# Part B's input rows by a plain transfer and a VectorE turn, with the late rows kept in SBUF

## The chip, the cores and the metric

The kernel runs on one core of a Trainium2 chip. The metric is the device time of one execution in microseconds. The core has a matrix engine (TensorE, PE in the profile, with its weight loads shown apart as PEld), VectorE (DVE), ScalarE (ACT), GpSimd (POOL) and SyncE (SP). All of them work on SBUF, which has 128 partitions; TensorE writes its sums to PSUM. Sixteen DMA engines move data between DRAM and SBUF. A transfer is issued from the instruction queue of one of the engines, here SyncE's or GpSimd's, and an engine that waits before issuing holds everything behind it in its queue.

## The reference

The output has two halves of 640 columns for 2048 tokens. Part A is a dilated sliding-window attention and is done first; the change touches its end only through a few copies. Part B is a recurrence over 64 segments of 32 tokens:

```python
for s in range(n_seg):                     # 64 segments, seg_len 32, memory of 8 rows
    xs = x[:, s * seg_len:(s + 1) * seg_len, :]
    h = concatenate([mem, xs], axis=1)     # 40 rows of 640
    q, k, v = h @ Wq, h @ Wk, h @ Wv       # 32 heads of 192
    p = softmax(where(mask, q k^T * scale, -1e9))
    o = (p v) @ Wo                         # 40 rows of 640
    mem = o[:, :8, :]
    outs.append(o[:, 8:, :])
```

All of it is bf16 with sums in fp32. The four weights of part B take 31.5 MB, more than SBUF holds. Each segment needs all of them, and needs the memory rows that the segment before it made.

## The kernel before, in words

Part B splits the 32 heads into four groups of eight. The weights are cut into units: for q, k and v a unit is 128 of the 640 input rows by the 1536 columns of a group, for the output weight a unit is 256 rows by 640 columns. Most units are loaded once and stay in SBUF. The 23 units per segment that `STREAMED` names are loaded anew in every segment into a ring of five buffers (`get_unit`, L387 to L395), from copies that part A made in DRAM. Their loads stand in SyncE's queue in the order of use; each waits until TensorE has read its buffer for the last time.

The 40 rows of a segment are split in an unusual way. 32 rows are "main": the 8 memory rows and the first 24 of the segment's x rows. The last 8 x rows are "late". A projection (`project32`, L445) multiplies 32 rows at a time, as stationary operand, with 384 weight columns, four column blocks side by side in the array. The late rows of four segments together make another block of 32 rows, "ahead". Since late rows don't depend on the memory, each weight group is projected for them only in one segment out of four (`RENEW`, and for q in `segment`, L640 to L650), for four segments at once. The result is turned on VectorE (`turn_late`, L472) and stored by GpSimd into small buffers, from which GpSimd later copies 8 columns per head into the q and k tiles (L491).

The input of a projection must have the 640 channels on partitions: a tile `HX` of 128 partitions, 5 channel blocks and 64 rows, 32 main and 32 ahead. There are two of these tiles, used in turn. To fill them, part A copies x in DRAM into `xwindows`, with 64 rows for every segment (`copy_windows`, L339): the 8 late rows of the segment before as placeholder for the memory, 24 main rows, and the 8 late rows each of four segments, placed so that the late rows of segment t always stand at position t modulo 4. `load_x(s)` (L429) is one transposing transfer of a window of 64 by 640 on SyncE's queue. It is called at the start of the segment before, and it stands between the loads of the last output units and those of the first k units.

At a segment's end the last group's output projection finishes in `Y`. Two engines copy it to `row` (L466, L467), TensorE turns the 8 memory rows (`memory_rows`, L592), and VectorE writes them over the placeholder in the next HX (L595). Only then can the next segment's first main projection start. In between TensorE projects ahead rows for q. The 32 other rows go out by two transfers on GpSimd's queue (L652). `row` shares its tile with the softmax values (`t` in the profile), so the first softmax of the next segment (L523) waits until the output transfer has read it.

TensorE's order in part B is the order of the program (`manual_schedule`, L657); the orders on the other engines are made by a scheduler. GpSimd also clears the old columns of P (L539) after the last turn of P in a segment.

Of the kernel before, what the change touches and what calls it, by code (L numbers as in the profile page):

```python
# [8 lines left out]
BF16 = mybir.dt.bfloat16  # L9
# [262 lines left out]
def part_b(ctx, tc, B_x, B_mem0, B_Wq, B_Wk, B_Wv, B_Wo, out, ident, n_seg, pre, nbuf, mid):  # L272
    nc = tc.nc
# [52 lines left out]
    def load_resident(units, engs):  # L326
        for k, u in enumerate(units):
            engs[k % len(engs)].dma_start(unit_tile(res[u], u), unit_src(u))
# [5 lines left out]
    respool = ctx.enter_context(tc.tile_pool(name="b_res", bufs=1))  # L334
    place_resident(respool, resident[:n_pre])
    dpool = ctx.enter_context(tc.tile_pool(name="b_copy", bufs=1, space=bass.MemoryType.DRAM))
    XW = dpool.tile([n_seg, 2 * SEG, Dm], BF16, name="xwindows")

    def copy_windows():  # L339

        rows = [(XW[0, 0:M], mem2[0:M]), (XW[0, M:SEG], x2[0:SEG - M])]
        for a, b in ((1, 49), (49, n_seg)):
            rows.append((XW[a:b, 0:SEG], x2[SEG * a - M:SEG * b - M].rearrange("(s n) d -> s n d", n=SEG)))
        groups = x2.rearrange("(t n) d -> t n d", n=SEG)[:, SEG - M:SEG]
        groups = groups.rearrange("(m k) n d -> k m n d", k=4)
        windows = XW[:].rearrange("(m k) n d -> k m n d", k=4)
        for r in range(4):
            for i in range(4):
                dst = windows[r][:, SEG + M * i:SEG + M * i + M]
                if i >= r:  # L350
                    rows.append((dst, groups[i]))
                else:
                    rows.append((dst[0:n_seg // 4 - 1], groups[i][1:n_seg // 4]))
                    rows.append((dst[n_seg // 4 - 1], groups[i][n_seg // 4 - 1]))
        for dst, src in rows:
            nc.sync.dma_start(dst, src)

# [10 lines left out]
        return ctx.enter_context(tc.tile_pool(name=name, reuse_waits="tile", **kw))  # L368

    xpool = pool("b_hx", bufs=1)  # L370
    HXs = [xpool.tile([128, 5, 64], BF16, name=f"HX{i}") for i in range(2)]
    wstream = pool("b_ws", bufs=nbuf)
    early = resident[n_pre:n_pre + 9]
    respool1 = pool("b_res1", bufs=1)
# [52 lines left out]
        (nc.scalar.copy if copies["n"] % 2 else nc.vector.tensor_copy)(dst, src)  # L427

    def load_x(s):  # L429
        if s < n_seg:  # L430
            nc.sync.dma_start_transpose(HXs[s % 2][:], XW[s])

    def main(s):
        return HXs[s % 2][:, :, 0:SEG]

    def ahead(s):
        return HXs[s % 2][:, :, SEG:2 * SEG]

    def columns(w, m, j):

# [4 lines left out]
    def project32(Xs, m, g, dcs=range(5), ps=None):  # L445

        if ps is None:
            ps = [ps_acc.tile([128, 384], FP32, tag="acc", name=f"acc{n}") for n in range(len(Xs))]
        for dc in dcs:
            w = get_unit((m, g, dc))  # L450
            for n, X in enumerate(Xs):
                for j in range(4):
                    nc.tensor.matmul(ps[n][32 * j:32 * j + 32, :], lhsT=X[:, dc, :], rhs=columns(w, m, j),  # L453
                                     start=(dc == 0), stop=(dc == 4), tile_position=(0, 32 * j))
        return ps
# [25 lines left out]
    def project_qk(s, m, g):  # L481
        T = tokens(QT if m == "q" else KT)
        renew = s == 0 or f"{m}{g}" in RENEW[s % 4]
        ps = project32([ahead(s), main(s)] if renew else [main(s)], m, g)
        if renew:
            turn_late(ps[0], m, g, s)
        sb = to_sb(ps[-1])

        def turns():
            b = late.pop((m, g, s))  # L490
            nc.gpsimd.tensor_copy(T[:, :, 32:L], b[:])  # L491
            free.append(b)
            turn(T[:, :, 0:32], sb)

        return turns

    def values(s, g):
        renew = s == 0 or f"v{g}" in RENEW[s % 4]
        ps = project32([ahead(s), main(s)] if renew else [main(s)], "v", g)
        for t, p in ((LV[g], ps[0]), (Vst, ps[-1]))[0 if renew else 1:]:  # L500
            v = t[:].rearrange("p (n e) -> p n e", e=64)
            w = bass.AP(v.tensor, v.offset, [v.ap[0], [256, 2], [1, 192]])
            evacuate(w, p[:].rearrange("p (h e) -> p h e", h=2))
# [55 lines left out]
    def mix(g, PT):  # L559

        ps = [ps_x.tile([128, 3, L], FP32, tag="x", name=f"OTps{a}") for a in range(4)]
        plan = [(late, half, k, col) for late in range(2) for half in range(2)
                for k, col in (((0, 0), (1, 128)), ((2, 320), (1, 192)))[half]]
        for n, (late, half, k, col) in enumerate(plan):
            V = LV[g] if late else Vst
            for a in range(4):
                nc.tensor.matmul(ps[a][:, k, :], lhsT=V[32 * a:32 * a + 32, col:col + 128],  # L567
                                 rhs=PT[32 * a:32 * a + 32, late, half, :],
                                 start=(n == 0), stop=(n == len(plan) - 1), tile_position=(32 * a, 0))
        for a in range(4):  # L570
            evacuate(OT[:, 3 * L * a:3 * L * a + 3 * L], ps[a][:].rearrange("p k n -> p (k n)"))

    def project_out(Y, g, pairs=range(6)):
        for a in pairs:
            i = 6 * g + a
            w = get_unit(("o", i, 0))
            for r in range(2):
                c = 2 * a + r
                for gv in range(2):
                    n = 640 * r + 320 * gv  # L580
                    nc.tensor.matmul(Y[64 * gv:64 * gv + 64, :], lhsT=OT[:, L * c:L * c + 64],  # L581
                                     rhs=w[:, n:n + 320], start=(i == 0 and r == 0), stop=(i == 23 and r == 1),
                                     tile_position=(0, 64 * gv))

    def memory_rows(s, Ysb):
        pt = ps_x.tile([128, 5, M], FP32, tag="x")
        for dc in (2, 0, 1, 3, 4):
            for gv in range(2):
                c0, c1 = max(128 * dc, 320 * gv), min(128 * dc + 128, 320 * gv + 320)
                if c0 < c1:  # L590
                    lo = c0 - 128 * dc
                    nc.tensor.matmul(pt[lo:lo + c1 - c0, dc, :], lhsT=Ysb[:, c0 - 320 * gv:c1 - 320 * gv],  # L592
                                     rhs=ident[:, 64 * gv:64 * gv + M], start=True, stop=True,
                                     tile_position=(0, lo))
        nc.vector.tensor_copy(HXs[(s + 1) % 2][:, :, 0:M], pt[:])  # L595

    def segment(s):
        last = s + 1 == n_seg
        load_x(s + 1)
        tq, tk, PT = {}, {}, {}  # L600
        tq[0] = project_qk(s, "q", 0)
        tk[0] = project_qk(s, "k", 0)
        tq[1] = project_qk(s, "q", 1)
        tq[0]()
        tk[0]()
        tk[1] = project_qk(s, "k", 1)
        put_p(s, 0, *softmax(scores(0)))
        tq[1]()
        tk[1]()
        tq[2] = project_qk(s, "q", 2)  # L610
        values(s, 0)
        soft = softmax(scores(1))
        tq[2]()
        PT[0] = turn_p()
        put_p(s, 1, *soft)
        tk[2] = project_qk(s, "k", 2)
        mix(0, PT[0])
        values(s, 1)
        tk[2]()
        PT[1] = turn_p()  # L620
        Y = ps_y.tile([128, 320], FP32, tag="y")
        project_out(Y, 0)
        put_p(s, 2, *softmax(scores(2)))
        tq[3] = project_qk(s, "q", 3)
        tk[3] = project_qk(s, "k", 3)
        mix(1, PT[1])
        values(s, 2)
        tq[3]()
        tk[3]()
        PT[2] = turn_p()  # L630
        project_out(Y, 1, range(0, 4))
        put_p(s, 3, *softmax(scores(3)))
        project_out(Y, 1, range(4, 6))
        mix(2, PT[2])
        values(s, 3)
        project_out(Y, 2, range(0, 4))
        PT[3] = turn_p(2)
        project_out(Y, 2, range(4, 6))
        mix(3, PT[3])
        if not last:  # L640
            gl = (s + 1) % 4
            ql = project32([ahead(s + 1)], "q", gl, range(0, 3))
        project_out(Y, 3)
        row = one.tile([128, 4, L], FP32, tag="t1")
        Ysb = row[:].rearrange("p a n -> p (a n)").bitcast(BF16)
        halves(Ysb, Y[:], 160)
        if not last:
            project32([ahead(s + 1)], "q", gl, range(3, 5), ql)
            memory_rows(s, Ysb)
            turn_late(ql[0], "q", gl, s + 1)  # L650
        for gv in range(2):
            nc.gpsimd.dma_start(out2[SEG * s:SEG * s + SEG, Dm + 320 * gv:Dm + 320 * gv + 320],  # L652
                                Ysb[64 * gv + M:64 * gv + L, :])

    load_x(0)
    load_resident(early, [nc.sync])
    with tc.manual_schedule(engines={mybir.EngineType.PE}):  # L657
        for s in range(n_seg):
# [71 lines left out]
```

## Time and profile before

| | |
|---|---|
| median of 3 runs | 2038.78 us (2033.06 to 2039.54) |
| profiled execution | 2035.72 us, span 2033.9 us |
| mean granted TensorE clock | 0.978 |
| busy: PE, DVE, ACT, POOL | 89%, 54%, 34%, 16% |
| DMA | 596 MB, 293 GB/s over the span |
| streamed loads per segment | 8 units of k, 5 of v (384 KB each), 10 of o (320 KB each) |
| median from issue to landing: k, v, o loads | 4.9, 5.0, 4.4 us |
| median from issue to landing: transpose of a window, output transfer | 4.6, 4.9 us |

Busy time says how much of the span an engine worked. A list of waits says for an engine and line what it waited for, how long in total, how often, and the longest wait. The chain is followed back from the last instruction and shows what set the end. An order of time shows single engines: start, length, line, operation, and in brackets the idle time before it and what ended it. SPq and POOLq are the instruction queues of SyncE and GpSimd, where issuing a transfer takes time too. The profile covers one execution; the shares are means over part A (the first 177 us) and the 64 segments.

### The profile page before, as it was taken

Reading aid. Unit: us, or ns where it says so; the run is one execution under the profiler, and the core shown is the slowest. Engines: PE = TensorE matmul, PEld = TensorE weight load, DVE = VectorE, ACT = ScalarE, POOL = GpSimd, SP = SyncE. Lnnn points to the kernel's source line nnn. Section 1 sums busy time; section 2 is a strip of 40 time slices with the busy share of each in tenths; the row PEclk is TensorE's granted clock in tenths of the full one; section 3 lists DMA queues with packets and bytes.
Section 4 is the critical chain, followed back from the end, with each engine's and each line's share of the span. In section 5 each row is a group of like instructions: output and inputs, shape, how many; then the busy total and the mean of one; then the engine's idle time right before and its main releaser. Section 6 shows DMA issues by size and latency. Waiting matters only on the chain.

```text
span 2033.9 us, 93689 instructions
## 1 busy us (share of the span) xinstructions
PE 1813.5 (89%) x40702; PEld 1136.7 (56%) x40702; DVE 1095.9 (54%) x3491; ACT 684.3 (34%) x1931; POOL 325.8 (16%) x1274
## 2 busy tenths in 40 slices
PE   7988888899888998999898988989898988998898
PEld 4655555555555555555555555555555554555555
DVE  5876455455555555555555455545554554455554
ACT  3544233333333333333333333333333332333332
POOL 2001111111111111121111111111111111111111
PEclk9999999999999999999999899999999999999999
DMA  9927998988999899999899899999998988999997
GB/s 345 305 76 271 311 292 298 296 296 295 292 301 311 292 300 304 315 304 303 297 310 307 277 294 306 311 290 298 301 304 291 302 289 280 295 291 305 309 301 261
DMA packets 270111, 596.07 MB, mean 293 GB/s; under 512 B 61065, under 2 KB 72841, under 8 KB 269385
## 3 DMA queue, kind: packets, MB, share of 16 engines
q1 hardware_dynamic: 264770, 585.97, 87.4%
q8 instruction: 319, 5.23, 1.0%
q0 software_dynamic: 4928, 4.11, 0.6%
q14 instruction: 94, 0.77, 0.1%
HBM read 576.85 MB, written 18.87 MB: 293 GB/s over the span
## 4 chain that ended last, share of the span: by engine, by line
PE 48%; DMA 26%; DVE 15%; issue 4%; ACT 4%; POOL 1%; SPq 1%; DVEq 0%; ACTq 0%; POOLq 0%
PE acc L453 21%; PE Y L581 16%; DMA t<-wcopy_o 11%; DMA out_dram<-row 7%; DMA t<-wcopy_v 3%; DVE QT L463 2%; PE OTps L567 2%; PE Sps L516 2%; DMA t<-wcopy_k 2%; DVE KT L463 2%; PE pq L95 2%; PE pt L550 2%; ACT sb L459 2%; DVE sm L531 1%; ACT t L529 1%
## 5 line engine op out<-in xcount | busy, mean ns | idle before, releaser
L453 PEld LDWEIGHTS <-HX 128*32 128x32 bf16 x19380 | 477.6, 97 | 324.2 <-issue 79.0
L581 PEld LDWEIGHTS <-OT 128*64 128x64 bf16 x6144 | 316.5, 110 | 175.6 <-issue 48.2
L459 ACT CAST sb<-acc 128x384 bf16<-128x384 f32 x646 | 298.5, 477 | 335.2 <-PE acc L453 295.3
L453 PE MATMUL acc<-wres_q,HX 128*32 128x384 bf16 x6460 | 335.4, 330 | 18.8 <-DVE HX L595 18.3
L581 PE MATMUL Y<-wres_o,OT 128*64 128x320 bf16 x3584 | 343.1, 303 | 7.6 <-DVE OT L427 7.6
L453 PE MATMUL acc<-t,HX 128*32 128x384 bf16 x4200 | 322.5, 335 | 29.6 <-DMA t<-wcopy_v 14.7
L581 PE MATMUL Y<-t,OT 128*64 128x320 bf16 x2560 | 282.3, 305 | 33.6 <-DMA t<-wcopy_o 28.0
L453 PE MATMUL acc<-wres_v,HX 128*32 128x384 bf16 x4844 | 285.8, 337 | 0.0
L529 ACT ACTIVATE t<-t 128x160 f32<-128x160 f32 x256 | 86.3, 337 | 493.3 <-DVE t L528 491.7
L523 DVE SCALAR_TENSOR_TENSOR t<-Sps,mask 128x160 f32<-128x160 f32 x256 | 81.6, 319 | 286.7 <-PE Sps L516 216.4
L453 PE MATMUL acc<-wres_k,HX 128*32 128x384 bf16 x3876 | 230.8, 334 | 0.0
L491 POOL COPY QT<-Lb 128x96 bf16<-128x96 bf16 x256 | 69.0, 269 | 862.9 <-PE Sps L516 862.9
L463 DVE STREAM_TRANSPOSE QT<-sb 128x384 bf16<-128x384 bf16 x256 | 144.2, 563 | 72.9 <-ACT sb L459 72.8
L427 DVE CAST OT<-OTps 128x120 bf16<-128x120 f32 x512 | 121.5, 265 | 77.2 <-PE OTps L567 76.9
L463 DVE STREAM_TRANSPOSE KT<-sb 128x384 bf16<-128x384 bf16 x256 | 143.9, 562 | 28.9 <-ACT sb L459 28.9
L516 PEld LDWEIGHTS <-QT 128*64 128x64 bf16 (+1 forms) x4096 | 120.1, 109 | 67.8 <-issue 39.8
L516 PE MATMUL Sps<-KT,QT 128*64 128x40 bf16 (+1 forms) x4096 | 137.1, 188 | 16.9 <-POOL KT L491 8.2
L479 POOL COPY Lb<-late 128x96 bf16<-128x96 bf16 x524 | 117.1, 270 | 165.9 <-DVE late L463 163.8
L531 DVE TENSOR_REDUCE sm<-t 128x4 f32<-128x160 f32 x256 | 81.2, 317 | 106.5 <-ACT t L529 106.5
L427 ACT CAST OT<-OTps 128x120 bf16<-128x120 f32 x512 | 107.6, 263 | 88.5 <-PE OTps L567 87.8
L550 PE MATMUL pt<-ident,P 128*128 128x128 bf16 x384 | 60.5, 230 | 63.5 <-DVE P L541 62.6
L463 DVE STREAM_TRANSPOSE late<-sb 128x384 bf16<-128x384 bf16 x134 | 76.7, 573 | 61.3 <-ACT sb L459 61.0
(77 smaller groups left out, 1543.4 us busy)
## 6 DMA issues: line engine op xcount, KB each, us to landing
t<-wcopy_o SPq DMA_DIRECT2D x640, 320.0 KB, 4.4
t<-wcopy_k SPq DMA_DIRECT2D x512, 384.0 KB, 4.9
t<-wcopy_v SPq DMA_DIRECT2D x320, 384.0 KB, 5.0
wres_q<-in_B_Wq_dram SPq DMA_DIRECT2D x20, 384.0 KB, 7.0
wres_v<-in_B_Wv_dram SPq DMA_DIRECT2D x15, 384.0 KB, 7.8
wres_k<-in_B_Wk_dram SPq DMA_DIRECT2D x12, 384.0 KB, 7.8
wres_o<-in_B_Wo_dram SPq DMA_DIRECT2D x14, 320.0 KB, 7.5
wcopy_o<-in_B_Wo_dram SPq DMA_DIRECT2D x10, 320.0 KB, 8.4
```

The costliest lines, as they stand in the source:

```text
L427: (nc.scalar.copy if copies["n"] % 2 else nc.vector.tensor_copy)(dst, src)
L453: nc.tensor.matmul(ps[n][32 * j:32 * j + 32, :], lhsT=X[:, dc, :], rhs=columns(w, m, j), start=(dc == 0), stop=(dc == 4), tile_position=(0 ...
L459: nc.scalar.copy(sb[:], p[:])
L463: nc.vector.transpose(dst, sb[:].rearrange("p (c f) -> p c f", f=32))
L479: nc.gpsimd.tensor_copy(late[m, g, t][:], tmp[:, :, M * (t % 4):M * (t % 4) + M])
L491: nc.gpsimd.tensor_copy(T[:, :, 32:L], b[:])
L516: nc.tensor.matmul(Sps[64 * g2:64 * g2 + 64, a, :], lhsT=QT[lo:hi, L * cc:L * cc + 64], rhs=KTt[lo:hi, cc, :], start=(g2 not in seen), sto ...
L523: nc.vector.scalar_tensor_tensor(out=t1[:], in0=Sps[:], scalar=scale, in1=mask[:].unsqueeze(1).to_broadcast([128, 4, L]), op0=ALU.mult, op ...
L529: nc.scalar.activation(t1[:], t1[:], ACTF.Exp)
L531: nc.vector.tensor_reduce(out=sm[:], in_=t1[:], axis=AX.X, op=ALU.add)
L550: nc.tensor.transpose(pt[:, late, :], src, ident)
L581: nc.tensor.matmul(Y[64 * gv:64 * gv + 64, :], lhsT=OT[:, L * c:L * c + 64], rhs=w[:, n:n + 320], start=(i == 0 and r == 0), stop=(i == 23 ...
```

## The change

`xwindows` shrinks to 32 rows per segment: 24 main rows, and in place of the placeholder the 8 late rows of the segment three further on. One more window holds the late rows of the first four segments. The windows are filled by 7 copies in place of 26.

HX shrinks to 32 rows. A tile `HXa` holds the late rows of four segments all the time; the projections of ahead rows read it. `load_x(s)` becomes a plain transfer of a window on GpSimd's queue into one tile `Xn`. Its access pattern takes four blocks of 32 columns outermost, so that partition 32j + t holds row t's columns of block j for each of the 5 channel blocks, in pieces of 32 elements. VectorE then turns 32 by 32 blocks (`turn_x`), which leaves channels on partitions. `next_x(s)` turns Xn into the HX of s, and GpSimd copies the 8 late rows that came with it over the oldest ones in HXa. Before the first segment two loads and turns fill HXa and the first HX.

In the order of the built program, the scheduler puts the turn for the segment after the next behind the evacuation of the fourth value group, and the next load of Xn on GpSimd's queue ahead of the clearing of P (L539) and of the output transfers (L652). The copy into HXa waits for the last projection that reads the old late rows. The transpose leaves SyncE's queue. No other instruction changes its place.

```diff
-    XW = dpool.tile([n_seg, 2 * SEG, Dm], BF16, name="xwindows")
+    XW = dpool.tile([n_seg + 1, SEG, Dm], BF16, name="xwindows")
     def copy_windows():
-        rows = [(XW[0, 0:M], mem2[0:M]), (XW[0, M:SEG], x2[0:SEG - M])]
-        for a, b in ((1, 49), (49, n_seg)):
-            rows.append((XW[a:b, 0:SEG], x2[SEG * a - M:SEG * b - M].rearrange("(s n) d -> s n d", n=SEG)))
...
-                dst = windows[r][:, SEG + M * i:SEG + M * i + M]
...
+        xs = x2.rearrange("(s n) d -> s n d", n=SEG)
+        main_rows, late_rows = xs[:, 0:SEG - M], xs[:, SEG - M:SEG]
+        rows = [(XW[0, 0:M], mem2[0:M]), (XW[0, M:SEG], main_rows[0]),
+                (XW[n_seg].rearrange("(i n) d -> i n d", n=M), late_rows[0:4])]
+        for a, b in ((1, 31), (31, n_seg)):
+            rows.append((XW[a:b, M:SEG], main_rows[a:b]))
+        rows += [(XW[1:n_seg - 3, 0:M], late_rows[4:n_seg]), (XW[n_seg - 3:n_seg, 0:M], late_rows[n_seg - 3:n_seg])]
...
-    HXs = [xpool.tile([128, 5, 64], BF16, name=f"HX{i}") for i in range(2)]
+    HXs = [xpool.tile([128, 5, SEG], BF16, name=f"HX{i}") for i in range(2)]
+    HXa = xpool.tile([128, 5, 4, M], BF16, name="HXa")
+    Xn = xpool.tile([128, 5, SEG], BF16, name="Xn")
...
     def load_x(s):
-        if s < n_seg:
-            nc.sync.dma_start_transpose(HXs[s % 2][:], XW[s])
+        nc.gpsimd.dma_start(Xn[:], XW[s].rearrange("t (c j f) -> j t c f", j=4, f=32))
+
+    def turn_x(dst):
+        nc.vector.transpose(dst, Xn[:])
+
+    def next_x(s):
+        turn_x(HXs[s % 2][:])
+        if s:
+            nc.gpsimd.tensor_copy(HXa[:, :, (s + 3) % 4, :], HXs[s % 2][:, :, 0:M])
...
     def segment(s):
         last = s + 1 == n_seg
-        load_x(s + 1)
...
         mix(0, PT[0])
+        if not last:
+            load_x(s + 1)
...
         values(s, 3)
+        if not last:
+            next_x(s + 1)
...
+    load_x(n_seg)
+    turn_x(HXa[:].rearrange("p c i n -> p c (i n)"))
     load_x(0)
+    next_x(0)
```

The projections of ahead rows read `ahead` (a view of HXa) in place of `ahead(s)`, and `memory_rows` writes into `main(s + 1)`.

More of the change, by code (lines that the diff above doesn't have):

```diff
@@ L336, in part_b @@
     dpool = ctx.enter_context(tc.tile_pool(name="b_copy", bufs=1, space=bass.MemoryType.DRAM))
-    XW = dpool.tile([n_seg, 2 * SEG, Dm], BF16, name="xwindows")
+    XW = dpool.tile([n_seg + 1, SEG, Dm], BF16, name="xwindows")
     def copy_windows():
-        rows = [(XW[0, 0:M], mem2[0:M]), (XW[0, M:SEG], x2[0:SEG - M])]
-        for a, b in ((1, 49), (49, n_seg)):
-            rows.append((XW[a:b, 0:SEG], x2[SEG * a - M:SEG * b - M].rearrange("(s n) d -> s n d", n=SEG)))
[L344 to L348, printed above, removed]
-                dst = windows[r][:, SEG + M * i:SEG + M * i + M]
[L350 to L354, printed above, removed]
+        xs = x2.rearrange("(s n) d -> s n d", n=SEG)
[5 more added lines that the diff above has]
+        rows += [(XW[1:n_seg - 3, 0:M], late_rows[4:n_seg]), (XW[n_seg - 3:n_seg, 0:M], late_rows[n_seg - 3:n_seg])]
         for dst, src in rows:
@@ L429, in load_x @@
     def load_x(s):
-        if s < n_seg:
-            nc.sync.dma_start_transpose(HXs[s % 2][:], XW[s])
+        nc.gpsimd.dma_start(Xn[:], XW[s].rearrange("t (c j f) -> j t c f", j=4, f=32))
[5 more added lines that the diff above has]
+            nc.gpsimd.tensor_copy(HXa[:, :, (s + 3) % 4, :], HXs[s % 2][:, :, 0:M])
     def main(s):
-        return HXs[s % 2][:, :, 0:SEG]
-    def ahead(s):
-        return HXs[s % 2][:, :, SEG:2 * SEG]
+        return HXs[s % 2]
+    ahead = HXa[:].rearrange("p c i n -> p c (i n)")
     def columns(w, m, j):
@@ L483, in project_qk @@
         renew = s == 0 or f"{m}{g}" in RENEW[s % 4]
-        ps = project32([ahead(s), main(s)] if renew else [main(s)], m, g)
+        ps = project32([ahead, main(s)] if renew else [main(s)], m, g)
         if renew:
@@ L498, in values @@
         renew = s == 0 or f"v{g}" in RENEW[s % 4]
-        ps = project32([ahead(s), main(s)] if renew else [main(s)], "v", g)
+        ps = project32([ahead, main(s)] if renew else [main(s)], "v", g)
         for t, p in ((LV[g], ps[0]), (Vst, ps[-1]))[0 if renew else 1:]:
@@ L594, in memory_rows @@
                                      tile_position=(0, lo))
-        nc.vector.tensor_copy(HXs[(s + 1) % 2][:, :, 0:M], pt[:])
+        nc.vector.tensor_copy(main(s + 1)[:, :, 0:M], pt[:])
     def segment(s):
         last = s + 1 == n_seg
-        load_x(s + 1)
         tq, tk, PT = {}, {}, {}
@@ L641, in segment @@
             gl = (s + 1) % 4
-            ql = project32([ahead(s + 1)], "q", gl, range(0, 3))
+            ql = project32([ahead], "q", gl, range(0, 3))
         project_out(Y, 3)
@@ L647, in segment @@
         if not last:
-            project32([ahead(s + 1)], "q", gl, range(3, 5), ql)
+            project32([ahead], "q", gl, range(3, 5), ql)
             memory_rows(s, Ysb)
```

## The prediction

> **What bounds the kernel now.** I read the page's head first (busy shares, the tenths, the queue), then the stage table, then the chain, then who waited for whom, then the order of time on single engines around the transfer that the change replaces.
>
> ```profile
> PE 1813.5 (89%) x40702; PEld 1136.7 (56%) x40702; DVE 1095.9 (54%) x3491; ACT 684.3 (34%) x1931; POOL 325.8 (16%) x1274
> q1 hardware_dynamic: 264770, 585.97, 87.4%
> PE 48%; DMA 26%; DVE 15%; issue 4%; ACT 4%; POOL 1%; SPq 1%; DVEq 0%; ACTq 0%; POOLq 0%
> ...
> 204.00:2034.00 1830.00, 1636.12 (x38244) 1025.79 (x38238) 959.01 (x3321) 590.16 (x1740) 303.39 (x1199) 0.98 0.91 298
> ```
>
> TensorE is busy for 89%, and the DMA engines for 91% of part B (last line: from 204 us on; columns are length, busy us of PE, PEld, DVE, ACT and POOL, clock, DMA share, GB/s). Both are nearly full, and the chain changes between them: 48% PE, 26% DMA, 15% VectorE. A part-B segment takes 28.8 us (the 63 first memory-row matmuls of L592 are that far apart on average). So a microsecond matters only where TensorE really stands still, and those places are few:
>
> ```profile
> DVE t L523 <- DMA out_dram<-row: 66.9, 33, 3.3
> PE pt L550 <- DVE P L541: 62.6, 75, 1.5
> PE Y L581 <- DMA t<-wcopy_o: 28.0, 46, 1.9
> PE acc L453 <- DMA t<-wcopy_v: 14.7, 22, 1.2
> POOL out_dram L652 <- DVE row L467: 282.4, 63, 8.7
> SPq L431 <- PE Y L581: 40.7, 33, 2.1
> ```
>
> Columns are the total wait, how often, the longest. In 33 of 63 segments the first softmax step waits for the output transfer of the segment before (2.0 us each), since both use one tile. TensorE waits some 52 us for streamed weights (o 28, v 15, k 9). By the TensorE timeline, counted from L592's first matmul, 34.6 of them lie between 27 us and 9 us of the next segment, a stretch of 12 us: 13.1 on the last o units, 9.0 on k, 12.5 on v. The other 17 us hold 15. This dense stretch is where the x transfer runs now:
>
> ```profile
> 926.73 1.72 SPq L394 DMA_DIRECT2D t<-wcopy_o  x2
> 928.78 1.62 SPq L431 DMA_TRANSPOSE HX<-xwindows  x1
> 930.50 3.43 SPq L394 DMA_DIRECT2D t<-wcopy_k  x4
> ...
> 930.12 0.13 POOL L539 MEMSET P<- 128x32 bf16 x1 [3.46 <-PE pt L553]
> 934.39 0.98 POOL L652 DMA_DIRECT2D out_dram<-row  x2 [4.14 <-DVE row L467]
> ...
> 928.79 0.56 DVE L427 CAST Vst<-acc 128x384 bf16<-128x384 f32 x1
> 931.14 0.47 DVE L427 CAST OT<-OTps 128x120 bf16<-128x120 f32 x2 [1.79 <-PE OTps L567]
> ```
>
> The first three are SyncE's queue: the transpose holds it for 1.2 to 1.6 us, with four k loads behind. Then GpSimd and VectorE in the same microseconds.
>
> **The change, part by part.** The sum is made against the profiled execution, 2035.7 us (span 2033.9 and 1.8 around it), 3.1 under the median of the three runs, 2038.8.
>
> *Removed: 64 transposes on SyncE's queue.* Each holds the queue for 1.21 us (median) and moves 320 packets of 256 bytes, median 18 ns in the packet records. In the first, second and third microsecond after its packets begin, 65, 40 and 83 weight packets start, against about 110 in the others. k0's first load could go when its buffer is free, about 929.7 instead of 930.5; the second gains 0.3 us, the rest wait for buffers anyway. What is it worth? At most the excess of the dense stretch over the rest of the segment: 34.6 - 12 x 0.9 = 24 us, of which 10 on o and 13 on k and v. The o part counts in full. The k and v part counts where the softmax is not late anyway, 30 of 63 segments: 6. I take -17; ends 0 (the buffers set the pace, not the transpose) and -24.
>
> *Added: 65 loads of Xn on GpSimd's queue.* In the built order each is issued right after VectorE has turned the piece before, a whole segment ahead of its use, behind HXa's copy and ahead of the clearing of P (L539) and the two output transfers (L652). Landing late therefore costs nothing; occupying GpSimd or the DMA engines may. GpSimd: a transfer of 32 rows takes it 0.50 us, one of 128 rows 0.55; by that slope 640 pieces take 0.8 us. Proportional to pieces, 0.50 x 640/32 = 9.9 us. I take 0.8 (the only slope there is), issued near 929.7 and done well before 934.4: cover 4.4 us, cost 0. Without the cover, the output transfer lands later and the 33 waits of 2.0 us grow.
>
> DMA engines: 640 pieces of 64 bytes. A 4-byte packet takes 9 ns, a 256-byte one 18; I take 13.5 per piece. The bytes matter less than how many engines share them, and the trace of before has no such pattern. The source is walked as four blocks of 32 columns outermost, so the ends are 4 engines with 160 pieces, 2.2 us each (1.4 to 2.9), and 16 engines with 40 pieces, 0.5 us each (0.4 to 0.7). Output transfers start their first packet 3.1 us after issue (median), so Xn's come at 932.8, amid the loads of k0's second unit and k1, and a load has landed only when its slowest engine has. k loads were late in 25 segments (0.36 us each), so I give them 1.0 us of slack. With four engines k1 is 1.2 us late; scores of the first group stand behind k1, so TensorE loses it, but in the 33 segments where softmax waits 2.0 us for the output anyway the loss is covered. 30 x 1.2 = +36. Ends: 0 (0.5 us is under the slack) and 2.9 x 30 = +87 (no slack). I take four, since nothing but the block count divides the outermost step.
>
> The Trainium skill ("DMA: Bandwidth & Descriptors", section "Why a DMA increments its semaphore by 16 and not by 1") says that a transfer uses the largest number up to 16 that divides the slowest dimension of both sides, but that some plain GpSimd copies go by partitions on all 16. By the rule the sum is as below, by the exception 36 us less; no run here shows either yet.
>
> *Added on VectorE: 65 turns.* A turn of 384 columns takes 563 ns, so one of 160 about 0.28 (ends 0.20, the 128x40 cast, and 0.56). 63 stand after the evacuation of the fourth value group, in the 1.79 us of idle shown above: 0. Two of the first three stand in the last softmax of part A, each behind a fresh load: +0.6, and up to +5 if the loads take 6 us; TensorE is 3 us behind there with its own sums.
>
> *Added on GpSimd: 63 copies into HXa*, 128x40, about 0.2 us, between the clearing (0.13) and the 128x96 copy (0.27). They wait for the last matmul that reads the old late rows. Behind them stand the copies of k's late rows, which come later by themselves; the first reader, the next q projection, is 2 us off at the least. 0. The memory rows of L595 now wait for this copy too, long done.
>
> *Part A:* 26 copies into the windows become 7 on SyncE's queue (25 us of issue), but the transfer behind them then waited 5.5 us for TensorE, so an earlier start buys nothing; 0, at most -2. The orders of ScalarE, and of everything not named, are unchanged.
>
> Sum: -17 + 36 + 0.6 = about +20, 2055 by the profiled execution, 2058 by the median.
>
> **Rivals.** *Few pieces per engine (ends on the other side).* If all 16 engines share Xn, its 0.5 us is under the slack and only the removal counts: -17 + 0.6, 2022. For it: every visible transfer with many rows is spread. Against: the four outermost blocks. It decides at -17 against 30 x (share - 1.0): below 1.6 us on the busiest engine the change gains.
>
> *Hidden anyway.* Buffers, not the transpose, set the loads, and the covered segments swallow the rest: within 6 us of 2039. For it: SyncE waits 713.7 us on TensorE's projections for buffers. Against: the dip in packets.
>
> *GpSimd writes the pieces slowly.* From 6.9 ns per piece (4.4 us / 640) the output transfers are held. At 8 us for a load: 3.6 x 33 + 2.6 x 30 = 197, less 17: 2219. For it: 640 pieces where no transfer of before has over 128. Against: 0.05 us for 96 more rows.
>
> *Each small piece costs like a large one.* The Trainium skill (same page, section "Specifications") gives 512 bytes as the least for full rate. As a mechanism here: between 18 ns (256 bytes) and 32 (640), 512 bytes take 27; 160 x 27 = 4.3 us; 30 x 3.3 + 33 x 1.3 = 142, less 17: 2164. Against: the 9-ns packets.
>
> **How the numbers follow.** Four engines 0.40 (own range 2035 to 2109: from 1.4 us per engine, 30 x 0.4 = 12, to 2.9 us without slack), sixteen 0.36, hidden 0.14, slow writing 0.07, costly pieces 0.03. A measurement of this kernel can tell about 0.3% (6 us; the three runs span 0.32%) from no change. So faster 0.36, same 0.14, slower 0.50. The range goes from the removal's full bound, 2015, to the end of +87 without slack, 2109, and leaves out the last two cases and little of the others.
>
> **What would show it.** The dip of GB/s at the transpose is gone, and the waits of TensorE for the last o units fall from 13 us to about 3. Right: waits for k and v in the first 9 us grow by some 36 us, and Xn's packets lie on few engines over 2 us or more. Wrong towards faster: they shrink. GpSimd's record for Xn near 0.8 us, the output transfer still issued at once after the row copy: else the slow rival. HXa's copy should be waited for by nobody.

## The result and the profile after

The changed kernel took 2056.14 us in the median (10 runs, 2042.50 to 2060.97), the kernel before on the same chip 2038.89 (10 runs). The ratio is 1.008, 95% interval 1.0057 to 1.0103, which is 12 to 21 us slower. The profiled execution of the changed kernel has a span of 2054.9 us at a mean clock of 0.984 (before 2033.9 at 0.978).

The page's head, queues and chain by engine, after:

```profile
PE 1816.4 (88%) x40702; PEld 1133.3 (55%) x40702; DVE 1112.3 (54%) x3556; ACT 684.0 (33%) x1931; POOL 476.2 (23%) x1402
...
q1 hardware_dynamic: 241634, 578.14, 86.1%
q0 software_dynamic: 9088, 7.27, 2.4%
...
PE 44%; DMA 28%; DVE 13%; issue 3%; ACT 3%; POOL 1%; DVEq 0%; ACTq 0%; POOLq 0%
```

The stage from 204 us on, after (length, busy us of PE, PEld, DVE, ACT and POOL, clock, DMA share, GB/s):

```profile
204.00:2054.00 1850.00, 1637.79 (x38254) 1022.49 (x38250) 975.37 (x3384) 590.59 (x1742) 445.06 (x1323) 0.99 0.91 294
```

TensorE is as busy as before, in a stage that is longer. The DMA engines moved fewer bytes per second (294 against 298 GB/s) at the same share. GpSimd's own queue, q0, takes 2.4% of the engines' time where it had 0.6%, although it carries only 3.2 MB more. The memory-row matmuls of the segments are 29.12 us apart on average (28.79 before). The time went into these places, from the waits of the changed kernel:

```profile
DVE t L525 <- DMA out_dram<-row: 57.3, 23, 3.5
...
PE acc L455 <- DMA t<-wcopy_k: 41.6, 70, 1.4
...
PE Y L583 <- DMA t<-wcopy_o: 18.8, 37, 1.6
PE acc L455 <- DMA t<-wcopy_v: 16.0, 29, 1.4
...
DVE HX L429 <- DMA Xn<-xwindows: 8.0, 2, 5.8
```

The line for k, before:

```profile
PE acc L453 <- DMA t<-wcopy_k: 9.0, 25, 1.1
```

TensorE waited for k loads 25 times before, 9.0 us in all; now it waits 70 times, 41.6 us. By the TensorE timeline, 33.5 of those lie between 4 and 6 us into a segment (4.9 before). The waits for o fell from 28.0 to 18.8; those on the last o units, from 27 us on, from 13.1 to 6.5. The waits for v are about what they were. The last line is new: two of the first three turns wait for their loads at the end of part A.

GpSimd around one load of Xn, in order of time, after:

```profile
912.81 2.02 POOL L426 DMA_DIRECT2D Xn<-xwindows  x1 [2.54 <-DVE HX L429]
914.82 0.14 POOL L541 MEMSET P<- 128x32 bf16 x1
917.06 1.03 POOL L657 DMA_DIRECT2D out_dram<-row  x2 [2.10 <-DVE row L469]
```

The load holds GpSimd for 2.02 us, and yet GpSimd then stands idle for 2.10 us until `row` is there: what it issues next is not held up by it. The load is issued 24.7 us into a segment (median of 60). The records of its packets begin 3.6 us later and end 7.6 us after the issue (medians), and it counts as landed after 8.6. So it reaches into the first microseconds of the next segment, where the k loads are under way.

### The profile page after: what moved, and what is told of

The parts are those of the page before. It is cut to its first block, busy times and chain, and to the rows that moved or that the text cites. A ratio compares the mean times of both kernels' runs of the same rounds, so it can differ in the third digit from the quotient of the medians.

```text
span 2054.9 us, 93706 instructions
## 1 busy us (share of the span) xinstructions
PE 1816.4 (88%) x40702; PEld 1133.3 (55%) x40702; DVE 1112.3 (54%) x3556; ACT 684.0 (33%) x1931; POOL 476.2 (23%) x1402
## 4 chain that ended last, share of the span: by engine, by line
PE 44%; DMA 28%; DVE 13%; issue 3%; ACT 3%; POOL 1%; DVEq 0%; ACTq 0%; POOLq 0%
PE acc L455 20%; PE Y L583 17%; DMA t<-wcopy_k 10%; DMA t<-wcopy_o 8%; DMA out_dram<-row 7%; DMA t<-wcopy_v 3%; PE OTps L569 2%; PE Sps L518 2%; DVE QT L465 2%; DVE KT L465 2%; PE pt L552 2%; DVE sm L533 1%; ACT t L531 1%; ACT sb L461 1%; DVE P L543 1%
## 5 line engine op out<-in xcount | busy, mean ns | idle before, releaser
L455 PEld LDWEIGHTS <-HX 128*32 128x32 bf16 x15360 | 387.1, 97 | 289.6 <-issue 72.5
L455 PE MATMUL acc<-t,HX 128*32 128x384 bf16 x3328 | 284.4, 334 | 47.9 <-DMA t<-wcopy_k 33.0
L583 PE MATMUL Y<-t,OT 128*64 128x320 bf16 x2560 | 281.7, 305 | 24.5 <-DMA t<-wcopy_o 18.8
L455 PE MATMUL acc<-wres_q,HX 128*32 128x384 bf16 x5120 | 258.0, 328 | 23.5 <-DVE HX L597 23.1
L455 PE MATMUL acc<-wres_v,HX 128*32 128x384 bf16 x3840 | 266.2, 338 | 0.3
L455 PE MATMUL acc<-wres_k,HX 128*32 128x384 bf16 x3072 | 211.1, 331 | 0.0
L426 POOL DMA_DIRECT2D Xn<-xwindows x65 | 131.3, 2019 | 247.5 <-DVE HX L429 176.1
L518 PEld LDWEIGHTS <-QT 128*64 128x64 bf16 (+1 forms) x4096 | 119.2, 109 | 57.5 <-issue 32.6
L455 PEld LDWEIGHTS <-HXa 128*32 128x32 bf16 x4020 | 99.6, 96 | 84.3 <-issue 28.2
```

The lines of the kernel that those rows point to most:

```text
L426: nc.gpsimd.dma_start(Xn[:], XW[s].rearrange("t (c j f) -> j t c f", j=4, f=32))
L518: nc.tensor.matmul(Sps[64 * g2:64 * g2 + 64, a, :], lhsT=QT[lo:hi, L * cc:L * cc + 64], rhs=KTt[lo:hi, cc, :], start=(g2 not in seen), sto ...
```

## The experiments

Ratios are to the kernel before on the same chip. "Period" is the mean distance of the segments in the one profile of each kernel (before 28.79 us at a clock of 0.978, after 29.12 at 0.984). Executions with a higher clock are shorter: of the 29 of the kernel before that were run beside the copies in part A, the four at a clock of 0.980 or less took 2037 us on average, the six at 0.986 or more 2027. So where a ratio and a period disagree the ratio decides.

### The load on more engines: four transfers of 32 rows

```diff
-        nc.gpsimd.dma_start(Xn[:], XW[s].rearrange("t (c j f) -> j t c f", j=4, f=32))
+        for j in range(4):
+            nc.gpsimd.dma_start(Xn[32 * j:32 * j + 32], XW[s].rearrange("t (c j f) -> j t c f", j=4, f=32)[j])
```

> The changed kernel, but each window is loaded by four transfers, one per block of 32 columns, each to 32 partitions; the same 640 pieces of 64 bytes, in the same place of GpSimd's queue. Theory (few engines hold the pieces): the outermost step is now 32 rows, so the pieces lie on all 16 engines, some 0.5 us each instead of 2.2; TensorE's waits for k fall from 41.5 us to about 10 to 15, and the time to 2022 to 2030, ratio to before 0.992 to 0.996. Rival (GpSimd's 2.0 us per load and the later output transfers are the cause): four issues of at least 0.5 us hold GpSimd as long, so the ratio stays near 1.008. Rival (the pieces cost the same wherever they lie): also 1.008.

Measured: ratio 0.9949 (0.9922 to 0.9975), period 28.50 us at 0.986. The packet records show 64 packets of 640 bytes per window, ten pieces each: 16 per transfer. No record names an engine; that a load lies on sixteen engines or on four is read here and below from the number of equal packets. Groups, issues and waits of this kernel:

```profile
L427 POOL DMA_DIRECT2D Xn<-xwindows x260 | 151.2, 586 | 243.3 <-DVE HX L430 171.4
```

```profile
PE acc L456 <- DMA t<-wcopy_v: 27.9, 42, 1.7
PE Y L584 <- DMA t<-wcopy_o: 18.8, 30, 2.4
...
PE acc L456 <- DMA t<-wcopy_k: 4.7, 14, 1.0
```

GpSimd issues four times as many transfers and is busy longer per window (4 x 586 ns against 2019 ns), the pieces are the same 640 of 64 bytes, and the waits for k are gone. So neither GpSimd's issue time nor the pieces as such made the change slow. Spread over sixteen engines the same bytes make a kernel faster than before. Not all of the k waits are gained: TensorE's waits for v grow from 16.0 to 27.9 us. Those for k, v and o together fall from 76.4 to 51.4, by 25 us, which is about what the ratios differ by (0.0131, 27 us).

### One transfer, sixteen engines

The windows are stored in DRAM as four column blocks of 32 rows with the pieces 128 bytes apart, so that a single transfer of 128 outer steps still has 640 pieces of 64 bytes. Part A's copies that make them are GpSimd's and there are 20 of them. The program has them after the fourth transpose of x, but in the order of the built program GpSimd issues them between 13 and 57 us, long before it.

```diff
-    XW = dpool.tile([n_seg + 1, SEG, Dm], BF16, name="xwindows")
+    XW = dpool.tile([n_seg + 1, 4, SEG, 5, 64], BF16, name="xwindows")
...
-        nc.gpsimd.dma_start(Xn[:], XW[s].rearrange("t (c j f) -> j t c f", j=4, f=32))
+        nc.gpsimd.dma_start(Xn[:], XW[s].rearrange("j t c f -> (j t) c f")[:, :, 0:32])
```

> As e4, but the windows in DRAM are padded so that the 32-element pieces of a load can't join: one transfer on GpSimd's queue, 640 pieces of 64 bytes as in the change, in one uniform row of 640, so 40 to an engine on all 16. Theory (the number of engines): segments near 28.5 us as with four transfers, waits for k under 15 us, and a GpSimd record of about 0.8 to 1.0 us. Rival (one long transfer of 640 small pieces, whatever the engines): 28.9 us or more, waits for k over 25 us. Part A is slower than in the change by the small copies, some 3 to 8 us.

Measured: ratio 0.996 (0.9934 to 0.9986), waits for k 9.9 us (19 times). The records show 16 packets of 2560 bytes per window, 40 pieces each, and GpSimd's record falls to 912 ns:

```profile
L428 POOL DMA_DIRECT2D Xn<-xwindows x65 | 59.3, 912 | 246.0 <-DVE HX L431 167.3 <-DVE HXa L431 42.7 <-PE pq L95 22.3
```

```profile
PE acc L457 <- DMA t<-wcopy_k: 9.9, 19, 1.0
...
PE pq L95 <- DMA xT<-in_A_x_dram: 9.2, 1, 9.2
```

The period, 28.75, is longer than expected, at a lower clock (0.977) than with four transfers. The ratio and the waits for k say the same as four transfers did: with 640 pieces still in one transfer, but by their packets on sixteen engines, the loss is gone. Part B starts late here (182.8 us against 177.0). Beside the early copies the third transpose of x is issued at 71.5 us, in the changed kernel at 52.4, and TensorE waits for it (second line).

The two versions on sixteen engines differ from the changed kernel in time too. There the load's packets run from 28.2 to 32.5 us after a segment's start (medians), that is up to 3 us into the next one; with four transfers from 26.1 to 30.1, here from 26.5 to 28.5. No run separates the spread from this earlier end. That a load on four engines delays another stream where it stands much earlier (further below) speaks for the spread.

### Larger pieces

Column blocks in DRAM again, but packed, so that the load is 128 rows of 320 bytes, with GpSimd's 20 copies in part A.

```diff
-    XW = dpool.tile([n_seg + 1, SEG, Dm], BF16, name="xwindows")
+    XW = dpool.tile([n_seg + 1, 4, SEG, Dm // 4], BF16, name="xwindows")
...
-        nc.gpsimd.dma_start(Xn[:], XW[s].rearrange("t (c j f) -> j t c f", j=4, f=32))
+        nc.gpsimd.dma_start(Xn[:], XW[s].rearrange("j t (c f) -> (j t) c f", f=32))
```

> The changed kernel, but part A writes the windows in DRAM already as four column blocks, by 20 copies on GpSimd's queue in pieces of 64 bytes, so that a load is 128 pieces of 320 bytes, 8 to an engine. Theory: 8 x 18 to 32 ns is under 0.3 us per engine, so a part-B segment is as long as without loads (0.992 of before), and GpSimd's issue falls from 2.0 us to about 0.55; part A may lose up to 10 us to the small copies, so the ratio lies between 0.992 and 0.998. Rival (any load on GpSimd's queue ahead of the output transfers costs it): a segment stays at 29.1 us.

Measured: ratio 0.998 (0.9954 to 1.0006), period 28.47 us at 0.983, waits for k 7.0, GpSimd 570 ns per load. In part B it is as good as four transfers; part A gives it back (part B starts at 180.8 us; the copies are as early as in the run above, and TensorE waits 8.8 us for the third transpose). Pieces five times as large bring nothing visible over sixteen engines with small ones.

### No loads in the segments

From the third segment on Xn isn't loaded again, and the turns read what is there.

```diff
         mix(0, PT[0])
-        if not last:
+        if s == 0:
             load_x(s + 1)
```

> The changed kernel without the loads of Xn from the third segment on, so all later segments compute on the x rows of the second; turns and copies into the late rows stay. Theory (the load alone costs, about 36 us): 2022, ratio to before 0.992, waits for k near those of before or less (9 us or below). Rival (the turn, the copy or the smaller tiles cost it): the ratio stays near 1.008.

Measured: ratio 0.9913 (0.9883 to 0.9942), period 28.37 us at 0.989, waits k 9.2, v 18.2, o 15.4. Against the changed kernel's 1.008 the loads cost 0.0167, some 34 us (26 to 42, both intervals taken together). The two profiles differ by 63 x 0.75 = 47 us, part of which is the higher clock here. By waits, 32.4 us of it is k:

```profile
PE acc L455 <- DMA t<-wcopy_k: 9.2, 19, 1.3
```

### The kernel before without its transposes

```diff
-        load_x(s + 1)
+        if s == 0:
+            load_x(s + 1)
```

> The kernel before without the transposes of windows from the third segment on, so later segments compute on the x rows of the first two; nothing else is changed. Theory (the removal is worth 17 us, at most 24): 2022, ratio 0.992 (0.988 to 0.995), with the waits for the last o units falling from 13 us to about 3 to 7. Rival (hidden anyway, buffers set the loads): ratio 0.998 to 1.002.

Measured: ratio 0.9937 (0.9913 to 0.9962), that is 13 us (8 to 18); period 28.54 us at 0.986, 63 x 0.25 = 16 us.

```profile
PE acc L453 <- DMA t<-wcopy_v: 20.1, 30, 1.7
PE Y L581 <- DMA t<-wcopy_o: 16.6, 39, 1.3
PE acc L453 <- DMA t<-wcopy_k: 12.7, 22, 1.5
```

Of the three streams only o gains (28.0 to 16.6); k and v wait a little more than before. The wait of the first softmax for the output transfer also falls (66.9 to 49.9).

### The late rows alone

HX of 32 rows, HXa, and windows of 32 rows as in the change, but loaded by a transposing transfer on SyncE's queue as before. No Xn and no turn.

```diff
-        nc.gpsimd.dma_start(Xn[:], XW[s].rearrange("t (c j f) -> j t c f", j=4, f=32))
+        nc.sync.dma_start_transpose(HXa[:].rearrange("p c i n -> p c (i n)") if s == n_seg else HXs[s % 2][:], XW[s])
...
-        turn_x(HXs[s % 2][:])
...
         last = s + 1 == n_seg
+        if not last:
+            load_x(s + 1)
...
         mix(0, PT[0])
-        if not last:
-            load_x(s + 1)
...
-    turn_x(HXa[:].rearrange("p c i n -> p c (i n)"))
```

> One part of the change alone: windows of 32 rows, late rows kept in HXa with GpSimd's copy, but the window still comes by a transpose on SyncE's queue, straight into HX; no Xn, no turn on VectorE. Theory (the transpose is worth 16 us, half by its packets and half by holding SyncE's queue): half the packets, the same hold, so a segment of 28.6 to 28.75 us against 28.79 before, and 3 to 6 us less in part A where there are fewer copies ahead of the last transposed block of A's x: ratio 0.993 to 0.998. Rival (the late rows kept in SBUF are themselves worth the 0.16 us by which e2's segments are shorter than e7's): 28.5 us or less, ratio below 0.993.

Measured: ratio 0.9959 (0.9928 to 0.9989), period 28.69 us at 0.983, waits for o from 27 us on 9.1. Part B starts at 169.6 us in place of 177.0, and these 7.4 us are nearly all of the gain (8.3 by the ratio). A transpose of half the rows and the copy into HXa move the segments by little. What pays here is part A.

### The copies in part A

That start was not in the prediction, so the kernel before was run with its 26 copies issued behind the fourth transpose of x, which they stand ahead of. Nothing else changes.

```diff
-    emit_loads(turn_x)
+    late_copies = emit_loads(turn_x)
...
             turn_x(3)
+            late_copies()
...
-        copy_windows()
+        return copy_windows
```

> The kernel before, with the 26 copies into the windows issued after the last transposed block of part A's x instead of ahead of it; all else as before. Theory (the copies held that block back and TensorE waited 5.9 us for it): the wait is gone, part B starts 4 to 6 us earlier, ratio 0.997. Rival (hidden, as the prediction had it): part B starts at 177 us as before, ratio 0.999 to 1.001.

Measured: ratio 0.9953 (0.993 to 0.9976). Part B starts at 169.6 us. SyncE's queue, first in the kernel before, then in this one:

```profile
82.73 24.98 SPq L356 DMA_DIRECT2D xwindows<-in_B_x_dram  x25
107.82 2.98 SPq L49 DMA_TRANSPOSE xT<-in_A_x_dram  x1
```

```profile
81.88 8.09 SPq L49 DMA_TRANSPOSE xT<-in_A_x_dram  x1
90.01 0.59 SPq L357 DMA_DIRECT2D xwindows<-in_B_mem_dram  x1
90.64 22.65 SPq L357 DMA_DIRECT2D xwindows<-in_B_x_dram  x25
```

In the kernel before, TensorE waited for that transfer, once and for 5.9 us:

```profile
PE pq L95 <- DMA xT<-in_A_x_dram: 5.9, 1, 5.9
```

This line is in none of the profiles that have few or late copies on SyncE's queue: not in that of the changed kernel either, which issues the transpose at 91.33. The two versions with copies on GpSimd's queue have it, but for the third transpose.

### The load at another place

A one-column GpSimd operation that reads Xn and the sum of the second softmax keeps the load behind that softmax.

```diff
         soft = softmax(scores(1))
+        if not last:
+            nc.gpsimd.tensor_tensor(held[:], Xn[:, 0, 0:1], soft[1][:, 0:1], op=ALU.mult)
```

> The changed kernel with a small GpSimd operation that reads Xn and a sum of the second softmax ahead of each load, so the load on four engines comes 8 to 14 us into a segment instead of at its end. Theory (the held engines cost only where a weight load in flight has no slack, which is k's second group at a segment's start): waits for k fall from 41.5 us to under 15, waits for weights between 12 and 20 us into the segment rise, and the ratio lies between 0.995 and 1.004. Rival (the held engines cost the same wherever the load stands): ratio near 1.008. Rival (it is the output transfers behind the load): ratio below 0.995.

Measured: ratio 1.1785 (1.1749 to 1.1822), span 2389.4 us at a clock of 0.924, period 34.5. The ratio is outside everything that was expected. VectorE, in order of time:

```profile
922.66 0.24 DVE L423 COPY PT<-pt 128x160 bf16<-128x160 bf16 x1
930.09 0.34 DVE L430 STREAM_TRANSPOSE HX<-Xn 128x160 bf16<-128x160 bf16 x1 [7.18 <-DMA Xn<-xwindows]
930.36 0.29 DVE L526 SCALAR_TENSOR_TENSOR t<-Sps,mask 128x160 f32<-128x160 f32 x1
```

The scheduler had put the turn ahead of the fourth softmax, and the load had just been issued, so VectorE stood for 7 us in each segment with that softmax behind it. The waits for k did fall, to 10.7 us. The run says nothing on the price of the place. What it shows is that the load needs its lead over the turn, which the change gives it.

### The same place, with the turn held back too

A second small operation writes a column of the next HX after the sum of the fourth softmax, and the turn overwrites it, so that it must come later.

```diff
-        put_p(s, 3, *softmax(scores(3)))
+        soft = softmax(scores(3))
+        put_p(s, 3, *soft)
...
         if not last:
+            nc.gpsimd.tensor_tensor(HXs[(s + 1) % 2][:, 0, 0:1], Xn[:, 0, 0:1], soft[1][:, 0:1], op=ALU.mult)
             next_x(s + 1)
```

> The changed kernel with two one-column GpSimd operations per segment: one reads Xn and the sum of the second softmax, so that the load of Xn can't be issued before that softmax (8 to 14 us into a segment, where TensorE hardly waits for weights); the other writes a column of the next HX after the sum of the fourth softmax, so that VectorE's turn stands behind that softmax, some 8 us after a load with 8.6 us of landing has ended. Place theory (the load on four engines costs because it meets the loads of k): TensorE's waits for k fall from 41.6 us to 8 to 14, no new wait for Xn, the mean distance of the segments falls from 29.12 to 28.4 to 28.6 us, ratio to the kernel before 0.991 to 0.998. Rival, a load on four engines delays whatever stream it meets: the waits turn up at v or o of the first groups, 28.85 to 29.1 us, ratio 1.000 to 1.009. Second rival, GpSimd: the 2.0 us of issue hold the copies of late rows into the q and k tiles behind it, so TensorE's waits for GpSimd (3.1 us in the changed kernel) grow to over 20 us and the ratio is over 1.003.

Measured: ratio 1.0075 (1.0045 to 1.0105), period 29.12 us at 0.984, both as in the changed kernel. The load is now issued 12.6 us into a segment (median). Waits of this kernel:

```profile
PE Y L584 <- DMA t<-wcopy_o: 34.9, 53, 2.0
...
PE acc L456 <- DMA t<-wcopy_v: 27.5, 33, 2.5
...
PE Sps L519 <- POOL KT L494: 20.8, 31, 0.7
...
PE acc L456 <- DMA t<-wcopy_k: 11.0, 23, 1.5
```

The waits for k went, as the place theory says, and came back elsewhere: 27.8 of the 34.9 us for o lie 19 to 22 us into the segment (3.9 in the changed kernel), just behind the load's packets, which run from 16.0 to 19.4 us. On top, TensorE waits 20.8 us for late rows that GpSimd copies (3.1 in the changed kernel). Of these 9.6 come 5 us into the segment, as with four transfers (9.5); the other 11.2, from 14 us on, come behind the load. Set beside four transfers, where k isn't late either, the waits for o are 16.1 us longer and those for late rows 11.3; the ratios differ by 0.0126, 26 us. Both rivals to the place theory were right in part, and the sum is the old one. Of the two places that were tried neither is free. By the waits, some 16 us of the price of the second come by way of o's loads and some 11 by way of GpSimd's queue, where the added operations stand too.

### Four transfers and late copies

The version that beats both kernels, with its copies into the windows also moved behind the fourth transpose of x. The diff is that of the four transfers with that of the copies.

> The version with four loads of 32 rows per window (ratio 0.9949 as it stood), and its seven copies into the windows issued behind part A's fourth transpose of x instead of ahead of it. Theory (the load's few engines were the loss, and in part A what stands ahead of the fourth transpose delays it): segments 28.4 to 28.6 us apart as with four loads, part B starts 1 to 4 us earlier than 173.9, ratio 0.991 to 0.996. Rival, part A's tail is set by the turns of the first windows on VectorE and not by the copies: start at 173.5 to 175, ratio 0.994 to 0.997.

Measured: ratio 0.9932 (0.9906 to 0.9958), median 2019.99 us, period 28.68 at 0.981. The period is above the 28.4 to 28.6 that were expected, at a lower clock than that of four transfers (0.985). Part B starts at 174.9 us, not earlier than the 173.9 of four transfers alone. The rival was right on that: seven copies hold that transpose up for some 7 us only, and the turns at the end of part A wait for Xn as before.

```profile
DVE HX L431 <- DMA Xn<-xwindows: 5.8, 2, 4.9
```

It is the fastest by its ratio of the versions that make all their loads, but its interval overlaps that of four transfers alone.

## Why the prediction was right

The predicted 2058 us is 1.9 us off the measured 2056.14, and what was named as the cause, a load with four outer steps that makes k late, is what the runs show. That the number came so near is luck: several terms were off and made up for each other.

**The load, +36.** Measured 34 us by the ratios (26 to 42), and k waits grew by 32.6 us. How it came about was predicted less well. In place of 1.2 us in 30 segments, the trace has k late in 51 of the 63, by 0.8 us on average; 29.4 of the 41.6 us lie in the 40 segments whose softmax doesn't wait for the output. Whether the engine time of 2.2 us holds stays open. In the records a load has 8 packets of 4096 and 4 of 2048 bytes, which is 64 + 64 + 32 pieces on each of four engines, and they take 3.3 us together (means), 0.8 per engine if there are four. To this come 24 packets of 256 bytes and 12 of 128, 4.7 us together, that the access pattern doesn't call for and that neither load on sixteen engines has. Their counts are 160 elements of 4 bytes for each of the twelve engines left over, or 480 for each of the four; the records name no engine, so that 0.8 us on the four or 2.0 is open. With 0.8 us per engine and the slack of 1.0 us the prediction's own sum would have come to nothing. So the term is right in size and in the stream that it hits, but the engine time, the slack and the cover that made it up are not borne out by the trace.

These counts fit the rule that the prediction weighed, from the Trainium skill ("DMA: Bandwidth & Descriptors", section "Why a DMA increments its semaphore by 16 and not by 1"): four outer steps, four engines. The exception for some plain GpSimd copies didn't apply here.

**The place, "amid the loads of k0's second unit and k1".** It was right on where the waits would be, and wrong in what it suggests. The last experiment but one has the load elsewhere and loses as much, in part by GpSimd's queue.

**The removal, -17.** Measured -13 by the ratio (-8 to -18) and -16 by the periods. The last o units were expected to fall from 13 us of waits to about 3, and fell to 6.5.

**GpSimd, 0.8 us and no cost.** The record is 2.02 us, 2.5 times as much, and the cost is still nothing where the load stands: 2.1 us of idle time follow it. The slope was taken from rows that a transfer has; the runs fit better with the number of pieces on an engine (below). Where the load was moved to stand ahead of GpSimd's copies, 11.2 us of TensorE's waits came behind it.

**VectorE's turns and HXa's copy, 0 in the segments.** Each turn took 335 ns (0.28 estimated) and HXa's copy 217 ns in the median; in the segments VectorE never waits for Xn, and no wait of TensorE names the copy. The output transfers, whose landing went from 4.9 to 5.4 us, made the first softmax wait 57.3 us in all where it was 66.9.

**Part A: this step was wrong, twice.** "An earlier start buys nothing; 0, at most -2": the transpose behind the copies was what TensorE waited for, 5.9 us, and moving the copies is worth 7.4 us at the start of part B. The prediction looked at the wait of the transpose for TensorE and not at TensorE's own wait for it, which is one line in the list. Against it stand the turns: "+0.6, and up to +5" was at its upper end or past it, for VectorE waits 2.27 and 5.77 us for the second and third load, and TensorE, whose sums need VectorE, then waits too:

```profile
151.46 0.33 DVE L429 STREAM_TRANSPOSE HXa<-Xn 128x160 bf16<-128x160 bf16 x1
...
157.84 0.34 DVE L429 STREAM_TRANSPOSE HX<-Xn 128x160 bf16<-128x160 bf16 x1 [2.27 <-DMA Xn<-xwindows]
...
167.39 0.34 DVE L429 STREAM_TRANSPOSE HX<-Xn 128x160 bf16<-128x160 bf16 x1 [5.77 <-DMA Xn<-xwindows]
```

Part B starts 3.1 to 7.9 us later in the four profiles that have the changed kernel's part A (172.7 to 177.5 us) than in that of the late rows alone (169.6). So the two errors nearly cancel, as far as single profiles that lie 5 us apart can tell.

With the measured sizes the sum is -13 + 34 - 7.4 + 5.5 (the middle of 3.1 and 7.9) = +19, against +16 measured (12 to 21). The first two terms have intervals of 5 and 8 us either way, so that the sum fits but proves little.

**The rivals.** "Few pieces per engine" would give 2022, a ratio of 0.992: four transfers gave 0.9949 and one on sixteen engines 0.996, so the price was near and only the condition didn't hold. "Hidden anyway" falls with the loads left out. "GpSimd writes the pieces slowly" needs 4.4 us of record and had 2.02, and four transfers hold GpSimd longer at no loss. "Each small piece costs like a large one" falls with the load of 320-byte pieces, which in part B does no better than small ones on sixteen engines, and with the packet records: 40 pieces of 64 bytes took 102 ns, not 40 times 27.

What stays open: what the extra packets are, on which engines they lie, and how much of the price is theirs. No run had four engines without them. Of a load's large packets at most four are under way at once in 53 of 60 loads, and five in the others; of the extra ones up to eleven are. This speaks for the twelve other engines but doesn't settle it, since more than 16 packets of all queues are under way at once in 18% of part B's time. Open too is how much the late start of the packets adds to the few engines.

## What to carry to other kernels

When a transfer shares the DMA engines with streams that are just in time, ask how it is spread before asking how many bytes it moves: 40 KB per segment with four outer steps cost 1.7% of the kernel here, and spread over sixteen engines 0.4%, no more than the intervals can tell. Moving it to a quieter stretch didn't help in the one place that was tried, where it delayed another stream and the copies behind it; dividing it, even into more instructions, did. And before costing an earlier transfer at nothing, look up who waits for it, not only what it waits for.

## What was not expected of the hardware

GpSimd's record for issuing a transfer goes by the pieces that fall to an engine, as far as these runs show: 0.50 us for the 32-row transfers of the kernel before, 0.57 for 128 pieces of 320 bytes, 0.59 for 160 pieces of 64 bytes on sixteen engines (ten each), 0.91 for 640 on sixteen (40 each), and 2.02 for 640 on four (160 each). Between the last three that is 9 to 11 ns per piece and engine.

A packet can hold many small pieces, and in the median the records show no price for them: 40 pieces of 64 bytes took 102 ns in the median, as much as a packet of 2560 bytes of an o load; 64 pieces took 159 ns at the 25th percentile, which is the same rate, and 233 in the median. The tails are long (750 and 770 ns at the 90th percentile), and with them the mean of 40 small pieces is 274 ns, against 179 for the same bytes in pieces of 320 bytes and 124 for an o load's packet. What makes the tail is open. The Trainium skill ("DMA: Bandwidth & Descriptors", section "Specifications") gives 512 bytes as the least transfer for full rate; the median packet of 40 pieces doesn't bear that out, and the mean leaves it open.

Leaving out 62 transposes of 80 KB, 320 packets of 256 bytes each, gained 13 us; SyncE's time for issuing them went with them. That is less than half of the 34 us that 62 loads of half the bytes on four engines cost.
